# An order for the row sums of the last attention pairs, three ties on VectorE, and two store queues in attention followed by two MLPs

## Chip, cores and metric

The kernel runs on 1 core of one Trainium2 chip. The metric is the device time of an execution in microseconds (us), the median of several runs.

## What is computed

Causal attention over 4 batches x 8 heads x 576 positions x 64 columns, with a cumulative bias on the scores, then an MLP with a leaky activation (its slope alpha is per hidden column), then an MLP with a squared ReLU. All in float32.

```
scores = scale * q @ k.T + minimum(-(cum_i - cum_j), 0), masked causally      # cum = cumsum(max(s, 0))
attn = exp(scores - max); attn = attn / (sum(attn) + 1e-9); out = attn @ v
x = out as [2304, 512]
h = x @ w_in;  g = max(h, 0) + alpha * min(h, 0);  x = g @ w_out               # 512 -> 2048 -> 512
h = x @ w_in2; r = max(h, 0);  g = r * r;          out = g @ w_out2            # 512 -> 2048 -> 512
```

A float32 matmul is made of three matmuls with operands split into a hi part (a cast on ScalarE) and a lo part (source minus hi, on VectorE): hi x hi, hi x lo, lo x hi (TERMS). So nearly every operand costs a cast and a VectorE subtraction, and a matmul with the lo part needs both.

## The kernel before

**Attention.** The 16 pairs of heads run as a software pipeline. PIPE lists 81 small steps with an offset in pairs; RAMP shifts single steps of single pairs by a fraction of a period; the sorted list is emitted step by step, and in_order() ties each instruction to the one before it on its engine, so that in this part every engine's order, SyncE's and GpSimd's included, is the written one. For a pair's row sums the steps are: fin (add eps, ScalarE), rec (line 438, reciprocal on VectorE), spr (line 443, a transpose on TensorE), v_spr (line 448, copy to SBUF on ScalarE), ds (lines 453 and 454, two stores to DRAM from SyncE), di (line 460, two broadcast loads into iv, which has a single buffer), nrm (lines 468 and 470, multiply x by iv on GpSimd). xa and xb (lines 524 and 540) are the products with v; both use one PSUM bank, so xb waits for the eviction of xa (line 278, ScalarE), which stands behind v_spr on ScalarE. After the step tr_4b of the last pair, 24 matmuls of the first MLP (early) are emitted.

**First MLP.** Three passes (c) of 768 tokens, each of 16 hidden blocks (f) of 128. From here the planner orders each engine's instructions by a timeline of its own; dependencies and explicit ties bind it. A step has 24 matmuls h = x @ w_in in two halves of 384 tokens (mlp_mm, line 591; each half has one PSUM bank, which the next step's same half takes over), the activation (mlp_act: lines 610 and 611 on VectorE for each half, then a cast and a subtraction of gs, lines 613 and 614), and, a step later, 24 matmuls of g @ w_out (mlp_out, line 874). Splits of the weights (lines 566 and 567) and conversions of weights for later (conv: lines 115 and 116 on ScalarE, 119 and 120 on VectorE, 124 on GpSimd, with scratch tiles cv_g and cv_t) run beside it, fed by loads of line 92. At the end of the last pass the order of f is 3 to 15, then 0, 1, 2; at f = 15 a list of eleven closures (x_steps: seven splits xc and four differences of x) is made, and in each later step of the loop up to four are taken from it. After the loop, what is left of it runs.

**Second MLP.** Three passes, each with a first product (stage1, line 996, seven products in Strassen's manner, with squares on GpSimd at line 1007) and a second product (Stage2, line 1126). Stage2 has 28 items (i, q): seven products i in the order 1, 5, 6, 2, 7, 4, 3, four q each. An item is 18 matmuls of 256 columns and needs a split th of g (split2, lines 910 and 911, three buffers). Items of i = 6, 7 and 4 (items 8 to 11, 16 to 19 and 20 to 23 of a pass) first need a difference of g in place, on VectorE (lines 1076, 1078, 1080); line 1031 makes one more at the end of stage1. In run, prepare(n + 2) is traced before item n's matmuls, and from n = 3 on every second item is followed by one step of x_steps for the next pass (none in the last). The results are stored by store (lines 1091, 1096, 1099); the last ones of the kernel are those of (mh, h) = (0, 1) with p = 2, in four issues.

`with tc.issue_after(a):` keeps each instruction traced in the block behind a in the order of a's engine. It adds no semaphore.

Of the kernel before, what the change touches and what calls it, by code (L numbers as in the profile page):

```python
# [19 lines left out]
def attention_then_two_mlps(  # L20
# [15 lines left out]
    P = 128  # L36
# [397 lines left out]
    def recip(n):  # L434

        sums = sums_of.pop(n)
        rs = rs_[n % 2][:, 0 : 2 * NT].rearrange("p (i h) -> p i h", h=2)
        nc.vector.reciprocal(rs, sums)
# [162 lines left out]
    def mlp_act(f, ph, first_block=False):  # L601
# [14 lines left out]

    gg_first = pp_.tile([P, HT], F32, name="gg_first")
# [136 lines left out]
    def emit(op, n):  # L754

        nonlocal lastpv, early, lasttr
# [46 lines left out]
        elif what == "rec":  # L803
            recip(n)
# [27 lines left out]
    RAMP = {("qk_10", 0): -0.911, ("qk_11", 0): -0.911, ("red_10", 0): -0.911, ("red_11", 0): -0.911, ("exp_10", 0): -0.911, ("exp_11", 0): -0.911, ("qk_00", 0): -0.964, ("red_00", 0): -0.964, ("qk_01", 0): -0.964, ("red_01", 0): -0.964, ("exp_00", 0): -0.964, ("exp_01", 0): -0.964, ("pp_q0", 2): 0.309, ("pp_q1", 2): 0.309, ("e_q0", 2): 0.309, ("e_q1", 2): 0.309, ("tr_3a", 0): -0.232, ("tr_3b", 0): -0.232, ("v_tr_3a", 0): -0.232, ("v_tr_3b", 0): -0.232, ("pp_k0", 2): 0.185, ("pp_k1", 2): 0.185, ("e_k0", 2): 0.185, ("e_k1", 2): 0.185, ("ppt", 3): -0.16, ("e_qt", 3): -0.182, ("v_xa", 4): -0.203, ("xb", 4): -0.181, ("exp_41", 4): -0.478, ("qk_40", 4): -0.478, ("qk_41", 4): -0.478, ("red_40", 4): -0.478, ("red_41", 4): -0.478, ("exp_40", 4): -0.478, ("qk_20", 4): 0.081, ("red_20", 4): 0.081, ("qk_21", 4): 0.081, ("red_21", 4): 0.081, ("exp_20", 4): 0.081, ("exp_21", 4): 0.081, ("tr_2b", 4): 0.031, ("v_tr_2b", 4): 0.031, ("tr_2a", 4): 0.031, ("v_tr_2a", 4): 0.031, ("e_kt", 3): -0.299, ("pp_k0", 4): -0.261, ("pp_k1", 4): -0.261, ("e_k0", 4): -0.261, ("e_k1", 4): -0.261, ("pp_q0", 4): 0.232, ("pp_q1", 4): 0.232, ("e_q0", 4): 0.232, ("e_q1", 4): 0.232, ("dk", 4): 0.103, ("lq", 3): 0.439, ("tr_2b", 0): -0.116, ("v_tr_2b", 0): -0.116, ("tr_2a", 0): -0.116, ("v_tr_2a", 0): -0.116, ("pp_k0", 1): -0.506, ("pp_k1", 1): -0.506, ("e_k0", 1): -0.506, ("e_k1", 1): -0.506, ("tr_4a", 0): -0.216, ("v_tr_4a", 0): -0.216, ("tr_4b", 0): -0.216, ("v_tr_4b", 0): -0.216, ("qk_10", 1): -0.054, ("qk_11", 1): -0.054, ("red_10", 1): -0.054, ("red_11", 1): -0.054, ("exp_10", 1): -0.054, ("exp_11", 1): -0.054, ("di", 2): -0.214, ("hi_k", 3): -0.711, ("exp_41", 2): -0.016, ("qk_40", 2): -0.016, ("qk_41", 2): -0.016, ("red_40", 2): -0.016, ("red_41", 2): -0.016, ("exp_40", 2): -0.016, ("lk", 2): 0.822, ("lw", 3): 0.44, ("ds", 1): 0.576, ("di", 3): -0.321, ("ppt", 2): 0.09, ("fin", 0): 0.036, ("v_spr", 1): 0.137, ("qk_20", 0): -0.121, ("red_20", 0): -0.121, ("qk_21", 0): -0.121, ("red_21", 0): -0.121, ("exp_20", 0): -0.121, ("exp_21", 0): -0.121, ("qk_10", 4): -0.044, ("qk_11", 4): -0.044, ("red_10", 4): -0.044, ("red_11", 4): -0.044, ("exp_10", 4): -0.044, ("exp_11", 4): -0.044, ("qk_20", 1): -0.084, ("red_20", 1): -0.084, ("qk_21", 1): -0.084, ("red_21", 1): -0.084, ("exp_20", 1): -0.084, ("exp_21", 1): -0.084, ("qk_00", 2): 0.032, ("red_00", 2): 0.032, ("qk_01", 2): 0.032, ("red_01", 2): 0.032, ("exp_00", 2): 0.032, ("exp_01", 2): 0.032, ("e_qt", 2): 0.056, ("ds", 2): 0.204, ("tr_4a", 3): -0.018, ("v_tr_4a", 3): -0.018, ("tr_4b", 3): -0.018, ("v_tr_4b", 3): -0.018, ("tr_2b", 2): 0.086, ("v_tr_2b", 2): 0.086, ("tr_2a", 2): 0.086, ("v_tr_2a", 2): 0.086, ("pp_k0", 3): 0.038, ("pp_k1", 3): 0.038, ("e_k0", 3): 0.038, ("e_k1", 3): 0.038}  # L832
# [25 lines left out]
    po = {}  # L858
# [3 lines left out]
    def mlp_out(c, f, gs, ws):  # L862
# [7 lines left out]
        for m in range(NKB):  # L870
# [91 lines left out]
    g_t = {}  # L962
# [22 lines left out]
    def stage1(stream, fill):  # L985
# [38 lines left out]
        def end(q):  # L1024
# [181 lines left out]
    for f in handed:  # L1206
        f()
# [59 lines left out]
```

## Time and profile before

| | us |
|---|---|
| median of 3 runs | 980.57 (979.06 to 980.58) |
| profiled execution | 979.85 |
| its span, first to last instruction | 978.1 |
| TensorE matmul busy | 954.1 |
| VectorE busy | 773.7 |
| ScalarE busy | 547.6 |
| GpSimd busy | 339.1 |

In the profile PE is TensorE's matmuls, PEld its weight loads, DVE VectorE, ACT ScalarE, POOL GpSimd, SPq and ACTq the DMA issues of SyncE and ScalarE. A row of a timeline has start, duration, engine, line, operation, output<-input; in brackets how long the engine had stood idle before it and what ended that. A row of the waits has who waited for whom, the total, the count and the longest. Attention runs to about 196 us, the first MLP to 608, the second in passes from 608, 733 and 855 to 973.

### The profile page before, as it was taken

Reading aid. Unit: us, or ns where it says so; the run is one execution under the profiler, and the core shown is the slowest. Engines: PE = TensorE matmul, PEld = TensorE weight load, DVE = VectorE, ACT = ScalarE, POOL = GpSimd, SP = SyncE. Lnnn points to the kernel's source line nnn. Section 1 sums busy time; section 2 is a strip of 40 time slices with the busy share of each in tenths; the row PEclk is TensorE's granted clock in tenths of the full one; section 3 lists DMA queues with packets and bytes.
Section 4 is the critical chain, followed back from the end, with each engine's and each line's share of the span. In section 5 each row is a group of like instructions: output and inputs, shape, how many; then the busy total and the mean of one; then the engine's idle time right before and its main releaser. Section 6 shows DMA issues by size and latency. Waiting matters only on the chain.

```text
span 978.1 us, 17664 instructions
## 1 busy us (share of the span) xinstructions
PE 954.1 (98%) x6451; PEld 899.7 (92%) x6451; DVE 773.7 (79%) x1399; ACT 547.6 (56%) x1152; POOL 339.1 (35%) x341
## 2 busy tenths in 40 slices
PE   7999999979999999999999999999999999999997
PEld 6888888869999999999999998998999999999997
DVE  7788878859888887778988768789967889677874
ACT  6999888835555543345645434565535645357442
POOL 7465644124333364442252310443003540035300
PEclk9999999999999999999999999999999999999999
DMA  5777754323444343434644532676544875448473
GB/s 150 190 192 206 191 148 128 83 90 130 129 129 129 101 160 139 144 124 147 233 160 130 183 119 101 185 251 239 179 172 148 290 236 191 171 124 267 138 240 132
DMA packets 107242, 161.39 MB, mean 165 GB/s; under 512 B 31730, under 2 KB 80498, under 8 KB 101778
## 3 DMA queue, kind: packets, MB, share of 16 engines
q1 hardware_dynamic: 106704, 159.89, 52.3%
q8 instruction: 51, 0.84, 0.4%
q10 hardware_dynamic: 450, 0.37, 0.1%
q14 instruction: 37, 0.30, 0.1%
HBM read 121.85 MB, written 30.11 MB: 155 GB/s over the span
## 4 chain that ended last, share of the span: by engine, by line
PE 87%; DVE 6%; DMA 3%; SPq 1%; issue 1%; ACT 1%; POOL 0%; ACTq 0%; POOLq 0%; DVEq 0%
PE ph L591 19%; PE po L874 18%; PE acc L1126 16%; PE b L996 5%; PE a L996 5%; PE ps_tr L490 5%; PE c L996 4%; PE ps_xa L524 2%; PE ps_sc L382 2%; PE ps_xb L540 2%; PE d L996 2%; PE ps_sc L383 2%; PE ps_tr L311 2%; PE ps_sc L388 2%; DVE xc L911 1%
## 5 line engine op out<-in xcount | busy, mean ns | idle before, releaser
L591 PE MATMUL ph<-xs,wi_hi 128*128 128x384 f32 x768 | 196.5, 336 | 5.7 <-DVE gg L611 5.7
L1126 PE MATMUL acc<-w2s,th 128*128 128x256 f32 x1512 | 186.5, 285 | 5.2 <-ACT th L910 3.7
L1126 PEld LDWEIGHTS acc<-w2s,th 128*128 128x128 f32 x1512 | 184.8, 193 | 6.4 <-ACT th L910 4.1
L874 PE MATMUL po<-gs,wo_hi 128*128 128x512 f32 (+1 forms) x768 | 167.6, 337 | 1.1 <-DVE xT L281 1.1
L591 PEld LDWEIGHTS ph<-xs,wi_hi 128*128 128x128 f32 x768 | 136.6, 188 | 8.3 <-DVE gg L611 6.4
L874 PEld LDWEIGHTS po<-gs,wo_hi 128*128 128x128 f32 x768 | 122.0, 189 | 15.5 <-DVE xT L281 1.3
L591 PE MATMUL ph<-xs,wi_lo 128*128 128x384 f32 x384 | 128.8, 335 | 0.0
L910 ACT CAST th<-g 128x768 fp32r<-128x768 f32 x84 | 69.8, 835 | 75.3 <-PE acc L1126 57.3
L911 DVE TENSOR_TENSOR th<-g,th 128x768 fp32r<-128x768 f32 x84 | 82.1, 983 | 25.2 <-ACT th L910 25.1
L613 ACT CAST gs<-gg 128x768 fp32r<-128x768 f32 (+1 forms) x48 | 39.8, 830 | 108.4 <-DVE gg L611 108.2
L874 PE MATMUL po<-gs,wo_lo 128*128 128x256 f32 (+1 forms) x384 | 99.5, 336 | 0.0
L124 POOL TENSOR_TENSOR wc<-cv_t,wc 128x512 uint32<-128x512 uint32 x32 | 47.5, 1487 | 143.5 <-DVE cv_t L120 98.1
L911 DVE TENSOR_TENSOR w1h<-w1f,w1h 128x512 fp32r<-128x512 f32 (+1 forms) x96 | 71.0, 746 | 23.1 <-ACT w1h L910 22.4
L1007 POOL TENSOR_TENSOR g<-g 128x384 f32<-128x384 f32 x24 | 22.2, 923 | 173.2 <-ACT g L1006 169.6
L610 DVE TENSOR_SCALAR gg<-ph,alpha_sb 128x384 f32<-128x384 f32 x95 | 58.0, 611 | 25.4 <-PE ph L591 25.0
L124 POOL TENSOR_TENSOR wf<-cv_t,wf 128x512 uint32<-128x512 uint32 x32 | 45.8, 1433 | 89.2 <-DVE cv_t L120 72.2
L910 ACT CAST w1h<-w1f 128x512 fp32r<-128x512 f32 (+1 forms) x96 | 53.6, 565 | 41.0 <-PE b L996 21.0
L614 DVE TENSOR_TENSOR gs<-gg,gs 128x768 fp32r<-128x768 f32 (+1 forms) x48 | 47.2, 983 | 37.0 <-ACT gs L613 37.0
L409 DVE CUSTOM_DVE_ANT_0 pr<-ps_sc,mask 128x128 f32<-128x128 f32 (+3 forms) x128 | 61.8, 486 | 14.8 <-PE ps_sc L383 11.8
L566 ACT CAST wi_hi<-wf 128x512 fp32r<-128x512 f32 x46 | 28.6, 622 | 78.7 <-PE ph L591 76.1
L591 PEld LDWEIGHTS ph<-xs,wi_lo 128*128 128x128 f32 x384 | 72.4, 188 | 0.1
L422 ACT ACTIVATE pr<-pr,nmax 128x128 f32<-128x128 f32 (+3 forms) x128 | 71.2, 557 | 0.4
(163 smaller groups left out, 2029.6 us busy)
## 6 DMA issues: line engine op xcount, KB each, us to landing
w2s<-w2D SPq DMA_DIRECT2D x42, 1024.0 KB
w1f<-w1D SPq DMA_DIRECT2D x72, 256.0 KB
raw_w<-in_moe_w_in_dram SPq DMA_DIRECT2D x32, 512.0 KB
w2D<-whl SPq DMA_DIRECT2D x16, 896.0 KB
raw_w<-in_moe_w_out_dram SPq DMA_DIRECT2D x24, 512.0 KB
w1D<-wc SPq DMA_DIRECT2D x8, 896.0 KB
iv<-sD SPq DMA_DIRECT2D x32, 144.0 KB
raw_q<-in_q_dram SPq DMA_DIRECT2D x16, 256.0 KB
```

Of the source, the lines that this page charges most:

```text
L124: nc.gpsimd.tensor_tensor(d, tt, d, ALU.add)
L409: nc.vector.tensor_tensor_reduce(o, banks.pop(("s", i, h))[:, :w], m, -1.0, first, ALU.add, ALU.min, nmax[:, h : h + 1])
L422: nc.scalar.activation(o, o, AF.Exp, bias=m, scale=-1.0, accum_out=sums_of[n][:, i, h : h + 1])
L490: last = nc.tensor.transpose(ps[:, z * P : (z + 1) * P], pr[:, c0 : c0 + P], ident)
L591: nc.tensor.matmul(ph[h][:, :HT], ws[a][:, kb * P : (kb + 1) * P], xs[kb][:, bb, h * HT : (h + 1) * HT], start=(cnt == 0), stop=(cnt == 3 ...
L610: nc.vector.tensor_scalar(x, ph[h][:, :HT], 0.0, alpha_sb[:, f : f + 1], ALU.min, ALU.mult)
L614: sub = nc.vector.tensor_sub(z[:, 1], a, z[:, 0].bitcast(F32))
L874: nc.tensor.matmul(acc, ws[a][:, m * P : (m + 1) * P], gs[:, bb, c_], start=first_ and z == 0, stop=lst and z == 2, skip_group_check=True,)
L910: a = nc.scalar.copy(dst[:, 0], src)
L911: v = nc.vector.tensor_sub(dst[:, 1], src, dst[:, 0].bitcast(F32))
L996: nc.tensor.matmul(pt[:, :HT], hl[:, a, c0 + kb * P : c0 + (kb + 1) * P], xc[i][:, b, kb, :], start=(first and cnt == 0), stop=(cnt == 5), ...
L1126: nc.tensor.matmul(acc[tb // 2][:, (tb % 2) * 256 : (tb % 2 + 1) * 256], th[:, x, qq, tb * P : (tb + 1) * P], ws[:, y, (2 * q + qq) % 4, : ...
```

## The change

Six edits. (1) RAMP has four more entries: di of pair 14 stands 0.57 of a period earlier, which is ahead of ds of pair 15 on SyncE; nrm 14 and di 15 and nrm 15 move up with it. (2) early is emitted after the turn (spr) of the last pair instead of before it. (3) In mlp_act, the lines 610 and 611 of a half are tied behind line 611 of the half before (behind the last reciprocal for the first). (4) A difference of g for an item of Stage2 is tied behind line 911 of the split of the item two before it. (5) Of the last stores, two of four are issued from ScalarE. (6) What is left of the eleven closures after the first MLP's loop is tied behind the last evictions on both engines. last_g is new and stores line 1031's instruction.

```diff
     def recip(n):
-        nc.vector.reciprocal(rs, sums)
+        return ins_of(nc.vector.reciprocal(rs, sums))
...
     def mlp_act(f, ph, first_block=False):
         for h in range(2):
             x = halves[h]
-            nc.vector.tensor_scalar(x, ph[h][:, :HT], 0.0, alpha_sb[:, f : f + 1], ALU.min, ALU.mult)
-            nc.vector.scalar_tensor_tensor(x, ph[h][:, :HT], 0.0, x, ALU.max, ALU.add)
+            with tc.issue_after(last_gg[0] or lastrec):
+                nc.vector.tensor_scalar(x, ph[h][:, :HT], 0.0, alpha_sb[:, f : f + 1], ALU.min, ALU.mult)
+            last_gg[0] = ins_of(nc.vector.scalar_tensor_tensor(x, ph[h][:, :HT], 0.0, x, ALU.max, ALU.add))
...
         elif what == "rec":
-            recip(n)
+            lastrec = recip(n)
...
-    RAMP = {..., ("e_k1", 3): 0.038}
+    RAMP = {..., ("e_k1", 3): 0.038, ("di", 14): -0.57, ("nrm", 14): -0.4, ("di", 15): -0.98, ("nrm", 15): -0.89}
...
-        if (op, n) == ("tr_4b", NP - 1):
+        if (op, n) == ("spr", NP - 1):
             early = mlp_mm(xs, first[0])
...
     def mlp_out(c, f, gs, ws):
-                    evac(xT[c][:, m, c_], acc, (m + z) % 2)
+                    last_out[(m + z) % 2] = evac(xT[c][:, m, c_], acc, (m + z) % 2)
...
             if q % 2:
-                nc.vector.tensor_sub(gq[:, :, 1], gq[:, :, 1], gq[:, :, 0])
+                last_g[0] = ins_of(nc.vector.tensor_sub(gq[:, :, 1], gq[:, :, 1], gq[:, :, 0]))
...
         def prepare(self, n):
-                if i == 6:
-                    nc.vector.tensor_sub(gq[:, :, 1], gq[:, :, 3], gq[:, :, 1])
-                elif i == 7:
-                    nc.vector.tensor_sub(gq[:, :, 0], gq[:, :, 1], gq[:, :, 0])
-                elif i == 4:
-                    nc.vector.tensor_sub(gq[:, :, 2], gq[:, :, 2], gq[:, :, 1])
+                if i in (6, 7, 4):
+                    a, b, c = {6: (1, 3, 1), 7: (0, 1, 0), 4: (2, 2, 1)}[i]
+                    with tc.issue_after(self.subs[-2]):
+                        nc.vector.tensor_sub(gq[:, :, a], gq[:, :, b], gq[:, :, c])
                 th = pools["m2"].tile([P, 2, 2, HT], F32R, name="th", tag="th", bufs=3)
                 self.last = split2(th, gq[:, :, PLACE[i]])
+                self.subs.append(self.last[1])
...
         def store(self, mh, h, y, tbs=range(3)):
+            e = nc.scalar if (mh, h) == (0, 1) else nc.sync
             for tb in tbs:
                 if rows[1] == rows[0] + TAIL:
-                    nc.sync.dma_start(out[rows[0] : rows[0] + P, cs], src)
+                    (e if tb == 2 else nc.sync).dma_start(out[rows[0] : rows[0] + P, cs], src)
                     continue
                 for z, r0 in enumerate(rows):
-                    nc.sync.dma_start(out[r0 : r0 + TAIL, cs], src[z * TAIL : (z + 1) * TAIL])
+                    (e if z else nc.sync).dma_start(out[r0 : r0 + TAIL, cs], src[z * TAIL : (z + 1) * TAIL])
...
-    for f in handed:
-        f()
+    with tc.issue_after(last_out[0]), tc.issue_after(last_out[1]):
+        for f in handed:
+            f()
```

## Rows read from the trace of the kernel before

**Rows 1.** The page: busy time of each engine, share of the span, instructions

```profile
PE 954.1 (98%) x6451; PEld 899.7 (92%) x6451; DVE 773.7 (79%) x1399; ACT 547.6 (56%) x1152; POOL 339.1 (35%) x341
```

**Rows 2.** TensorE's waits: who for whom, us in total, times, longest

```profile
PE ph L591 <- DVE gg L611: 5.7, 2, 4.2
PE acc L1126 <- ACT th L910: 3.7, 2, 1.8
...
PE acc L1126 <- DVE th L911: 1.5, 2, 0.8
PE po L874 <- DVE xT L281: 1.1, 1, 1.1
PE ps_xb L540 <- ACT xT L278: 0.9, 1, 0.9
```

**Rows 3.** Three stretches: us, busy time by engine (instructions), PEclk, DMA share, GB/s

```profile
221.10:224.50 3.40, 3.40 (x12) 3.21 (x11) 3.33 (x5) 3.04 (x6) 1.33 (x1) 0.50 0.28 100
...
685.30:688.70 3.40, 3.40 (x18) 3.40 (x17) 3.40 (x5) 1.73 (x3) 0.00 (x0) 0.51 0.00 0
...
690.00:733.00 43.00, 43.00 (x357) 43.00 (x357) 32.49 (x41) 19.39 (x26) 0.00 (x0) 1.00 0.60 199
```

**Rows 4.** Timeline of TensorE behind attention: start, us, instruction, idle before

```profile
207.18 0.62 PE L591 MATMUL ph<-xs,wi_hi 128*128 128x384 f32 x2 [1.51 <-DVE gg L611]
...
211.28 1.32 PE L874 MATMUL po<-gs,wo_hi 128*128 128x512 f32 x6
...
220.01 0.62 PE L591 MATMUL ph<-xs,wi_hi 128*128 128x384 f32 x2 [4.21 <-DVE gg L611]
```

**Rows 5.** Timeline of VectorE in the same stretch

```profile
205.71 0.62 DVE L610 TENSOR_SCALAR gg<-ph,alpha_sb 128x384 f32<-128x384 f32 x1 [3.29 <-PE ph L591]
...
206.58 1.02 DVE L611 SCALAR_TENSOR_TENSOR gg<-ph,gg 128x384 f32<-128x384 f32 x2
...
210.86 0.55 DVE L614 TENSOR_TENSOR gs<-gg,gs 128x384 fp32r<-128x384 f32 x1
...
215.66 0.43 DVE L119 TENSOR_SCALAR cv_t<-cv_g 128x512 uint32<-128x512 uint32 x1 [3.92 <-POOL wf L124]
...
219.41 0.55 DVE L611 SCALAR_TENSOR_TENSOR gg<-ph,gg 128x384 f32<-128x384 f32 x1
```

**Rows 6.** Timelines of GpSimd and of SyncE's queue in the same stretch

```profile
195.07 0.60 POOL L470 TENSOR_TENSOR xT<-xT,iv 128x192 f32<-128x192 f32 x1
206.70 1.01 POOL L468 TENSOR_TENSOR xT<-xT,iv 128x384 f32<-128x384 f32 x1 [11.03 <-DMA iv<-sD]
...
214.33 1.30 POOL L124 TENSOR_TENSOR wf<-cv_t,wf 128x512 uint32<-128x512 uint32 x1
...
202.92 6.91 SPq L460 DMA_DIRECT2D iv<-sD  x4
```

**Rows 7.** Timeline of VectorE at the end of pass 2 of the first MLP

```profile
606.38 0.95 DVE L911 TENSOR_TENSOR xc<-x,xc 128x768 fp32r<-128x768 f32 x1
```

**Rows 8.** Timelines of VectorE, GpSimd and TensorE at the start of Stage2, pass 0

```profile
677.98 0.95 DVE L1078 TENSOR_TENSOR g<-g 128x768 f32<-128x768 f32 x1
678.85 1.58 DVE L1076 TENSOR_TENSOR g<-g 128x768 f32<-128x768 f32 x1
...
682.95 0.95 DVE L1031 TENSOR_TENSOR g<-g 128x768 f32<-128x768 f32 x1
...
678.36 1.25 POOL L1007 TENSOR_TENSOR g<-u 128x384 f32<-128x384 f32 x1 [3.65 <-ACT u L1006]
...
684.87 5.34 PE L1126 MATMUL acc<-w2s,th 128*128 128x256 f32 x30 [1.83 <-ACT th L910]
```

**Rows 9.** Timelines of DMA issues: SyncE behind the last matmul, ScalarE at the start

```profile
973.49 1.11 SPq L1099 DMA_DIRECT2D out_dram<-k  x2
974.70 0.53 SPq L1096 DMA_DIRECT2D out_dram<-k  x1
...
1.23 0.48 ACTq L251 DMA_DIRECT2D raw_k<-in_k_dram  x1
```

More of the change, by code (lines that the diff above doesn't have):

```diff
@@ L615, in mlp_act @@
         return gs, ins_of(act), ins_of(sub)
+    last_gg, lastrec = [None], None
     gg_first = pp_.tile([P, HT], F32, name="gg_first")
@@ L754, in emit @@
     def emit(op, n):
-        nonlocal lastpv, early, lasttr
+        nonlocal lastpv, early, lasttr, lastrec
         what, _, a = op.partition("_")
@@ new lines, in attention_then_two_mlps @@
+    RAMP = {("qk_10", 0): -0.911, ("qk_11", 0): -0.911, ("red_10", 0): -0.911, ("red_11", 0): -0.911, ("exp_10", 0): -0.911, ("exp_11", 0): -0.911, ("qk_00", 0): -0.964, ("red_00", 0): -0.964, ("qk_01", 0): -0.964, ("red_01", 0): -0.964, ("exp_00", 0): -0.964, ("exp_01", 0): -0.964, ("pp_q0", 2): 0.309, ("pp_q1", 2): 0.309, ("e_q0", 2): 0.309, ("e_q1", 2): 0.309, ("tr_3a", 0): -0.232, ("tr_3b", 0): -0.232, ("v_tr_3a", 0): -0.232, ("v_tr_3b", 0): -0.232, ("pp_k0", 2): 0.185, ("pp_k1", 2): 0.185, ("e_k0", 2): 0.185, ("e_k1", 2): 0.185, ("ppt", 3): -0.16, ("e_qt", 3): -0.182, ("v_xa", 4): -0.203, ("xb", 4): -0.181, ("exp_41", 4): -0.478, ("qk_40", 4): -0.478, ("qk_41", 4): -0.478, ("red_40", 4): -0.478, ("red_41", 4): -0.478, ("exp_40", 4): -0.478, ("qk_20", 4): 0.081, ("red_20", 4): 0.081, ("qk_21", 4): 0.081, ("red_21", 4): 0.081, ("exp_20", 4): 0.081, ("exp_21", 4): 0.081, ("tr_2b", 4): 0.031, ("v_tr_2b", 4): 0.031, ("tr_2a", 4): 0.031, ("v_tr_2a", 4): 0.031, ("e_kt", 3): -0.299, ("pp_k0", 4): -0.261, ("pp_k1", 4): -0.261, ("e_k0", 4): -0.261, ("e_k1", 4): -0.261, ("pp_q0", 4): 0.232, ("pp_q1", 4): 0.232, ("e_q0", 4): 0.232, ("e_q1", 4): 0.232, ("dk", 4): 0.103, ("lq", 3): 0.439, ("tr_2b", 0): -0.116, ("v_tr_2b", 0): -0.116, ("tr_2a", 0): -0.116, ("v_tr_2a", 0): -0.116, ("pp_k0", 1): -0.506, ("pp_k1", 1): -0.506, ("e_k0", 1): -0.506, ("e_k1", 1): -0.506, ("tr_4a", 0): -0.216, ("v_tr_4a", 0): -0.216, ("tr_4b", 0): -0.216, ("v_tr_4b", 0): -0.216, ("qk_10", 1): -0.054, ("qk_11", 1): -0.054, ("red_10", 1): -0.054, ("red_11", 1): -0.054, ("exp_10", 1): -0.054, ("exp_11", 1): -0.054, ("di", 2): -0.214, ("hi_k", 3): -0.711, ("exp_41", 2): -0.016, ("qk_40", 2): -0.016, ("qk_41", 2): -0.016, ("red_40", 2): -0.016, ("red_41", 2): -0.016, ("exp_40", 2): -0.016, ("lk", 2): 0.822, ("lw", 3): 0.44, ("ds", 1): 0.576, ("di", 3): -0.321, ("ppt", 2): 0.09, ("fin", 0): 0.036, ("v_spr", 1): 0.137, ("qk_20", 0): -0.121, ("red_20", 0): -0.121, ("qk_21", 0): -0.121, ("red_21", 0): -0.121, ("exp_20", 0): -0.121, ("exp_21", 0): -0.121, ("qk_10", 4): -0.044, ("qk_11", 4): -0.044, ("red_10", 4): -0.044, ("red_11", 4): -0.044, ("exp_10", 4): -0.044, ("exp_11", 4): -0.044, ("qk_20", 1): -0.084, ("red_20", 1): -0.084, ("qk_21", 1): -0.084, ("red_21", 1): -0.084, ("exp_20", 1): -0.084, ("exp_21", 1): -0.084, ("qk_00", 2): 0.032, ("red_00", 2): 0.032, ("qk_01", 2): 0.032, ("red_01", 2): 0.032, ("exp_00", 2): 0.032, ("exp_01", 2): 0.032, ("e_qt", 2): 0.056, ("ds", 2): 0.204, ("tr_4a", 3): -0.018, ("v_tr_4a", 3): -0.018, ("tr_4b", 3): -0.018, ("v_tr_4b", 3): -0.018, ("tr_2b", 2): 0.086, ("v_tr_2b", 2): 0.086, ("tr_2a", 2): 0.086, ("v_tr_2a", 2): 0.086, ("pp_k0", 3): 0.038, ("pp_k1", 3): 0.038, ("e_k0", 3): 0.038, ("e_k1", 3): 0.038, ("di", 14): -0.57, ("nrm", 14): -0.4, ("di", 15): -0.98, ("nrm", 15): -0.89}
@@ L856, in attention_then_two_mlps @@
     ps_o = part1.enter_context(tc.tile_pool(name="ps_o", bufs=1, space=PSUM, reuse_waits="tile"))
-    po = {}
+    po, last_out = {}, {}
     ORD = [list(range(NF))] * (NPASS - 1) + [list(range(NPRE, NF)) + list(range(NPRE))]
@@ L960, in w2_slab @@
         return t
-    g_t = {}
+    g_t, last_g = {}, [None]
     W1_ORDER = []
@@ L1061, in __init__ @@
             self.items = [(i, q) for i in ORDER2 for q in range(NQ // 2)]
-            self.th, self.slab, self.done = {}, {}, 0
+            self.th, self.slab, self.done, self.subs = {}, {}, 0, []
         def fetch(self, i, hq):
```

1 line of the change is left out of this document (removed).

## The prediction

> **What bounds the kernel now.** I read the page first, then TensorE's waits, then the timelines around each wait. TensorE is busy 954.1 us of 978.1 [rows 1] and its chain of waits is short [rows 2]: some 11 us have another engine as their cause after the start, and they stand in four places. From 224.5 us to 602 us TensorE never stops, so an edit there can only lose. The places are: (A) the turn from attention to the first MLP, 200.8 to 220 us, where it waits 0.95 us for an eviction and 1.51 and 4.21 us for the activation of a half (gg, line 611); (B) the end of pass 2 at 606.6 us, 1.07 us for an eviction; (C) the start of the second product in pass 0 and again in pass 1, in all 3.7 us for ScalarE's split and 1.5 us for VectorE's (the pass that has no next x to prepare, the last, shows no such wait); (D) the last stores behind the last matmul. After the 4.21 us wait and after the first of the waits in C the granted clock stands at 0.50 and 0.51 for 3.4 us each [rows 3], the 1.2 GHz level.
>
> The wall of the change is therefore: A 6.67, B 1.07, C 5.13, the two slow stretches, and D. Two slow stretches lose at most half of 3.4, 1.7 us each; by the matmul count, 18 in 3.4 us against 357 in 43.0 us (0.120 each), it is 1.2. I take **1.5 each**.
>
> **A, the first two edits.** Why is gg late? Two causes, both in the rows. First, VectorE's order [rows 5]: the first step of gg for step 1 stands at 205.71, after 3.29 us of idling for its matmuls, *ahead* of the second step of the half before it, at 206.58. The older half's own first step came before that idling, and its bank is what TensorE waits for until 207.18 [rows 4]. Tying each half's first step behind the last half's second puts it into the idle time: the 1.51 us go. Second, GpSimd [rows 5, 6]: at 215.66 VectorE has stood 3.92 us before the second conversion step, because the sum of line 124 that frees its scratch tile runs only at 214.33, behind both last norms; and the gg steps that free TensorE at 220.01 are queued behind that instruction. The norms wait for their DMAs: SyncE issues all four loads of inverse sums in one row from 202.92 on, since the stores of pair 15 stand ahead of pair 14's loads, and those stores wait for the turn, which TensorE does after the 24 early matmuls.
>
> After the change: pair 14's loads go ahead of pair 15's stores, and issue when the norm of pair 13 leaves the single buffer, 195.67. From the second load's issue (203.46 in the row's stretch, half a microsecond into it) to the norm at 206.70 are 3.2 us; so issue 195.8, the norm 199.6 to 201.6. The turn comes before the early matmuls, so both stores are out by about 199, well before pair 15's loads at 201.7; its norm ends at 207.3 where it ended at 214.3. Seven microseconds of GpSimd are freed ahead of line 124. The four issues on SyncE's queue are only reordered; behind them wait the weight loads of line 92, which go earlier too. The transpose of the turn is the same one, moved, so TensorE pays nothing. The copy behind it runs under the early matmuls, and so does the eviction queued behind that copy on ScalarE, which was the 0.95 us. So 6.67 us and one slow stretch are gone, and I ask what is late next: the split activation gs of step 0. TensorE would be at its matmuls, 211.28 in the trace [rows 4], 2.46 us earlier, at 208.8. VectorE's last part of gs ends at 211.41; its run from 205.71 on starts 0.95 earlier and is shorter by the one 0.55 us instruction pulled ahead: 209.9. I charge **1.0 us** of new wait. Bounds: 0 if the weight splits fill the former idle time, and 3 if the next pair of gg steps (1.2 us) and GpSimd's overlap come in front. A = 6.67 + 1.5 - 1.0 = **7.2** (5 to 8.4).
>
> The tie costs nothing later: in the steady steps the second half's matmuls end 2 us after the first's, so the order is the one that stands there anyway. The tie of the first half to the reciprocal of pair 15 adds nothing, as the early matmuls now come behind that pair's turn.
>
> A rule speaks against moving the norms. In the trace a difference of two tiles on VectorE, 0.95 us otherwise, took 1.58 us beside a GpSimd product [rows 8]. The Trainium skill, "SBUF — State Buffer", section "Who interferes with whom", says that a VectorE instruction with two SBUF inputs and a GpSimd instruction that reads SBUF exclude each other for the whole instruction; the trace agrees by that 0.6 us. By it, pair 15's norm, now at 205.7 to 207.3 amid VectorE's busiest stretch, would cost up to two such delays, 1.2 us, and A would be 6.0.
>
> **C, the ties of the differences.** In pass 0, TensorE stops 0.70 us for item 6's split and then 1.83 us, until 684.87, for item 7's [rows 8]. VectorE isn't idle there: between 675 and 686 it runs six differences, for items 8, 9, 10, 16, 17 and 18, among them line 1078 at 677.98 (item 16) and line 1076 at 678.85 (item 9, 1.58 us, beside GpSimd). Line 1031, on which item 7's cast waits, is issued at 682.95 although GpSimd's product for it ended at 679.61. A difference for item m may now come only behind item m-2's split. Item 8's may stand behind item 6's, the other five not before item 7's. Four of the six stand ahead of line 1031, three at 0.87 us from start to start and one at 1.5 with the overlap: 4.1 us leave its front, and it can follow GpSimd at about 680; cast and split then end at 681.8, and the hi part is wanted at 681.9, when items 4 to 6 run through at 18 x 0.120 = 2.17 us each. Both waits go, in pass 1 alike.
>
> The differences don't vanish; they come where splits are due. No semaphore is added: a difference stands in VectorE's own order behind a split that waits for ScalarE's cast, which waits for one of three buffers; behind it are queued the next split and what prepares the next x. From 690 to 733 us VectorE is busy 32.5 of 43 us [rows 3]; six more at 0.95 make 38.2. Locally it is tight. Items 8 to 23 hold 16 splits, 12 differences, 8 steps for the next x and 6 sums of 0.55: 36 x 0.87 + 3.3 = 34.6 us, against TensorE's 16 x 2.17 = 34.7. With two items of lead less a cast and a split, 2.5 us, that holds; at 0.95 a piece it misses by 0.3. The last pass has no x steps, 28 x 0.87 + 3.3 = 27.7: no wait. I charge **0.7 us** over both passes. C = 5.13 + 1.5 - 0.7 = **5.9** (3 to 6.6).
>
> **D, the stores.** Behind the last matmul stand four issues on SyncE; the last pair starts at 973.49 (two in 1.11 us) and 974.70 (0.53) [rows 9]. Two of the four go to ScalarE's queue, which is empty by then. An issue there took 0.48 us at the kernel's start. So the last issue ends near 974.1 and not 975.23: **1.1 us** (0.5 if ScalarE's issue takes the 1.1 us that another at the start took). Passes 0 and 1 take the first branch of store, which is unchanged.
>
> **B, the last tie: nothing.** The eleven steps of x_steps are handed out four to a step of the loop, and three steps follow the one that makes them (f = 0, 1, 2): 12 places for 11. The list is empty when the tied loop starts. The 1.07 us, caused by the split at 606.38 [rows 7] between two evictions, stays. last_g is set and read nowhere. Bounds -1.07 to +1, since the planner lays every engine's order anew.
>
> **Sum**, against the profiled execution's 979.85 (span 978.1 and 1.75 around it): 7.2 + 5.9 + 1.1 = 14.2, giving 965.65. The median of the runs, 980.57, is 0.72 above that execution, so **966.3**.
>
> **The rivals.** (1) *The turn keeps a stall.* VectorE's backlog, not GpSimd, is the bound: for it, 1.0 us of wait came out of my own order; against, the 3.29 and 3.92 us that VectorE idles there [rows 5]. If TensorE still stops 3.5 us and the clock falls, A gives 3.2: 970.4. (2) *Line 1031 is late for another cause*, the chain sum, ScalarE, GpSimd; for it, the cast's wait names line 1031 and no difference; against, the 3.3 us between product and line 1031. C gives 1: 971.2. Both: 975.2. (3) *The planner's order comes out as before* where it matters, since a tie only sets a lower bound: 978.6 to 982.5. (4) *Slower: VectorE becomes the bound of the second product.* 36 pieces at s us in items 8 to 23, less the lead: at s = 1.1 it is 42.9 - 34.7 - 2.5 = 5.7 us late in each of two passes, with two slow stretches 14.4; less A and D, 986.7. It decides from s = 1.03, where the loss eats A and D. For it, 1.58 us beside GpSimd; against, GpSimd has no work at all from 690 to 733 [rows 3].
>
> **How the numbers follow.** Forecast, 963 to 968.5: 0.62. Rival 1 or 2 alone, 968.5 to 973: 0.20; both: 0.05; rival 3: 0.05; rival 4: 0.08. Faster by over 0.2% (2 us, about what a measurement of this kernel tells from no change): 0.87; within: 0.05; slower: 0.08. The lower end is all of A, C and D with no new wait, 964.7, and B's gap gone with it, 963.6, less spread; the range 963 to 974 leaves out rivals 3 and 4, half of "both", and a few hundredths below.
>
> **What would show it.** Right: no wait for gg at 205 to 220 and none for th at 680 to 685 and 803 to 808; the granted clock 1.00 from 26 to 973; line 124's first sum near 208; two stores on ScalarE's queue, SyncE's end about 1 us earlier behind the last matmul; the 1.07 us at the end of pass 2 still there. Wrong: a new wait for gs near 209, or for th in items 16 to 23.

## The result, and the profile of the changed kernel

| | before | after |
|---|---|---|
| median of the runs, us | 980.58 (979.06 to 981.55) | 966.94 (965.37 to 968.26) |
| profiled execution, us | 979.85 | 967.17 |
| its span, us | 978.1 | 965.4 |
| end of the last matmul, us | 973.07 | 961.27 |

The ratio of after to before is 0.9862, with an interval of 0.9842 to 0.9881. The forecast, 966.3 us, was met within 0.7 us, and faster was the likeliest case. The sum is right partly by luck, though: one term was too small, a small one was forecast as nothing, and a loss of 3.9 us that the text didn't see took their gains back. Against the profiled execution, for which the sum was made, it missed by 1.5 us (965.65 forecast, 967.17 measured).

TensorE's waits (who waits for whom, total us, times, longest) are to be read beside [rows 2]:

```profile
PE ph L591 <- DVE gg L612: 1.7, 1, 1.7
PE ph L591 <- DVE xs L578: 1.4, 2, 0.8
...
PE po L876 <- DVE xT L281: 0.5, 1, 0.5
```

(From line 637 on, a line of before has a number two higher in after; line 611 is now 612, and 910 and 911 are 912 and 913.) The waits of acc for th have gone, 5.2 us in all in [rows 2]; the waits for gg fell from 5.7 to 1.7; the wait of ps_xb is gone; po's fell from 1.1 to 0.5. One line behind the start is new: ph waits twice for xs.

**The turn.** TensorE's timeline (start, us, instruction, idle before it) has the place of [rows 4]:

```profile
206.11 1.33 PE L876 MATMUL po<-gs,wo_hi 128*128 128x512 f32 x6
209.14 0.62 PE L591 MATMUL ph<-xs,wi_hi 128*128 128x384 f32 x2 [1.69 <-DVE gg L612]
...
211.33 0.51 PE L876 MATMUL po<-gs,wo_hi 128*128 128x512 f32 x2
```

A wait near 209 was forecast, 1.0 us for gs; it came at 209.14, 1.69 us, for gg. Step 3 of the first MLP (the early matmuls are step 0), which started at 227.98 in before, starts at 220.61: 7.37 us earlier, of which 0.35 are already there when the early matmuls start. The change doesn't touch what stands ahead of them but for one transpose; over the twelve profiled executions of this document's kernels they start anywhere from 195.46 to 196.33 us.

GpSimd (answers to [rows 6]) and SyncE's queue show the mechanism as forecast:

```profile
199.09 1.01 POOL L468 TENSOR_TENSOR xT<-xT,iv 128x384 f32<-128x384 f32 x1 [3.75 <-DMA iv<-sD]
...
204.48 1.01 POOL L468 TENSOR_TENSOR xT<-xT,iv 128x384 f32<-128x384 f32 x1 [3.84 <-DMA iv<-sD]
205.45 1.05 POOL L470 TENSOR_TENSOR xT<-xT,iv 128x192 f32<-128x192 f32 x1
206.47 1.73 POOL L124 TENSOR_TENSOR wf<-cv_t,wf 128x512 uint32<-128x512 uint32 x1
...
195.36 1.08 SPq L460 DMA_DIRECT2D iv<-sD  x2
196.55 0.67 SPq L453 DMA_DIRECT2D sD<-rT  x1
197.26 0.61 SPq L454 DMA_DIRECT2D sD<-rT  x1
200.67 1.13 SPq L460 DMA_DIRECT2D iv<-sD  x2
```

Pair 14's loads go at 195.36, ahead of pair 15's stores at 196.55, and no longer in one row of four from 202.92. Its norm stands at 199.09 instead of 206.70, and line 124's first sum at 206.47 instead of 214.33 (near 208 was forecast).

**The start of the second product, pass 0.** VectorE, the answer to [rows 8]:

```profile
676.02 0.95 DVE L1033 TENSOR_TENSOR g<-g 128x768 f32<-128x768 f32 x1
676.89 0.95 DVE L1080 TENSOR_TENSOR g<-g 128x768 f32<-128x768 f32 x1
677.93 0.96 DVE L913 TENSOR_TENSOR th<-g,th 128x768 fp32r<-128x768 f32 x1
678.80 0.95 DVE L1080 TENSOR_TENSOR g<-g 128x768 f32<-128x768 f32 x1
679.67 0.95 DVE L913 TENSOR_TENSOR th<-g,th 128x768 fp32r<-128x768 f32 x1
680.54 0.95 DVE L1080 TENSOR_TENSOR g<-g 128x768 f32<-128x768 f32 x1
```

Line 1031 (now 1033) starts at 676.02 instead of 682.95, ahead of the differences. These (line 1080) and the splits (line 913) alternate, where [rows 8] has two differences in a row ahead of line 1031; and TensorE has no wait left there, in either pass.

**The new place.** At the end of pass 0 of the first MLP, TensorE's timeline and a stretch (us, busy by engine, PEclk, DMA share, GB/s):

```profile
328.80 0.33 PE L591 MATMUL ph<-xs,wi_hi 128*128 128x384 f32 x1
329.92 0.44 PE L591 MATMUL ph<-xs,wi_hi 128*128 128x384 f32 x1 [0.79 <-DVE xs L578]
...
331.31 0.44 PE L591 MATMUL ph<-xs,wi_hi 128*128 128x384 f32 x1 [0.60 <-DVE xs L578]
...
332.50:335.90 3.40, 3.40 (x12) 3.40 (x11) 3.40 (x7) 2.51 (x4) 0.00 (x0) 0.50 0.01 5
```

The first split of the next pass's x is late, twice, and then the granted clock stands at 0.50, the 1.2 GHz level, for 3.4 us, as it did behind the waits of [rows 3]; at 221.1 and at 685.3 us it is now 1.00.

**The gain by places**, from the starts of the same matmuls in both traces (a difference of differences, so what a wait does to the matmuls and the clock behind it is in it):

| stretch | gain, us | forecast |
|---|---|---|
| start, before the turn | 0.35 | 0 |
| A, the turn (to step 3) | 7.0 | 7.2 |
| end of pass 0 (step 16 to 17) | -3.86 | 0 |
| B, end of pass 2 | 0.6 | 0 |
| C, second product, pass 0 | 3.9 | 5.9 with pass 1 |
| C, pass 1 | 3.5 | |
| the last pass | 0.2 | 0 |
| D, behind the last matmul | 0.88 | 1.1 |
| sum (span) | 12.6 | 14.2 |

The span fell by 12.7, 1.5 less than the sum. The rest of the way to the forecast is the spread of the runs: after's median lies 0.23 us below its profiled execution, where before's lay 0.72 above.

### The profile page after: what moved, and what is told of

Its sections match the earlier page's. It is cut to its first block, busy times and chain, and to the rows that moved or that the text cites. A ratio compares the mean times of both kernels' runs of the same rounds, so it can differ in the third digit from the quotient of the medians.

```text
span 965.4 us, 17665 instructions
## 1 busy us (share of the span) xinstructions
PE 953.2 (99%) x6451; PEld 899.7 (93%) x6451; DVE 773.4 (80%) x1399; ACT 547.5 (57%) x1152; POOL 334.7 (35%) x341
## 4 chain that ended last, share of the span: by engine, by line
PE 80%; DVE 11%; issue 3%; ACT 2%; DMA 2%; SPq 1%; POOL 1%; ACTq 0%; DVEq 0%; POOLq 0%
PE acc L1128 18%; PE ph L591 14%; PE po L876 13%; PE a L998 5%; PE b L998 5%; PE c L998 5%; PE ps_tr L490 5%; PE ps_xb L540 3%; PE d L998 3%; PE ps_xa L524 2%; PE ps_sc L382 2%; PE ps_sc L383 2%; PE ps_tr L311 2%; PE ps_sc L388 2%; DVE gg L611 2%
## 5 line engine op out<-in xcount | busy, mean ns | idle before, releaser
L876 PE MATMUL po<-gs,wo_hi 128*128 128x256 f32 (+1 forms) x768 | 167.0, 336 | 0.5 <-DVE xT L281 0.5
```

Source lines behind the costliest of these rows:

```text
L876: nc.tensor.matmul(acc, ws[a][:, m * P : (m + 1) * P], gs[:, bb, c_], start=first_ and z == 0, stop=lst and z == 2, skip_group_check=True,)
```

## The experiments

Kernels built on before do one part of the change alone; kernels built on after add something to all six. Each time is beside the kernel before of the same batch of runs.

**The turn alone** (edits 1 and 2). The edit is the four new entries of RAMP and

```diff
-        if (op, n) == ("tr_4b", NP - 1):
+        if (op, n) == ("spr", NP - 1):
```

> The kernel before with edits 1 and 2 alone (loads of pair 14 ahead of the stores of pair 15; the turn ahead of the early matmuls). Theory: GpSimd's lateness behind the last two norms is the cause of the 4.21 us wait, so line 124's first sum comes near 207 and not 214, the 4.21 and the 0.95 us go and the slow stretch behind them too; VectorE's order of the halves is untouched, so a wait of about 1.5 us for gg near 205 to 208 stays: 4.5 to 7 us faster than before. Rival, the order of gg on VectorE is the cause of both waits: at most 1.5 us faster, and a wait of 3 us or more for gg between 205 and 220 is still there.

Measured: 972.67 us (971.83 to 975.02), ratio 0.9932 (0.9908 to 0.9955); that is 7.75 us below its before, more than the 4.5 to 7 expected. Its waits, and two rows of VectorE:

```profile
PE acc L1126 <- ACT th L910: 3.3, 2, 1.8
...
PE ph L591 <- DVE xs L578: 1.4, 2, 0.8
PE ph L591 <- DVE gg L611: 1.2, 1, 1.2
...
203.00 0.55 DVE L611 SCALAR_TENSOR_TENSOR gg<-ph,gg 128x384 f32<-128x384 f32 x1
204.02 0.62 DVE L610 TENSOR_SCALAR gg<-ph,alpha_sb 128x384 f32<-128x384 f32 x1 [0.47 <-PE ph L591]
```

Step 3 starts 8.1 us earlier than in before, 7.5 of them behind the start of the early matmuls. So the first two edits give all of A: the second step of a half (203.00) now comes ahead of the first step of the next (204.02) without a tie. Without edit 3 the wait for gg is 1.2 us, less than the 1.69 of after. The wait for xs at the end of pass 0 is here too, so it comes from the turn and from no other edit. It costs 2.3 us here, against 3.86 in after: the two waits are about equally long (0.83 and 0.59; 0.79 and 0.60), but here the granted clock stays at 1.00 behind them. The difference, **1.5 us, is what one half-clock stretch of 3.4 us costs**, as the prediction had estimated it. (From the starts of the matmuls in after's slow stretch itself it comes out at 1.6.)

**The activations' tie alone** (edit 3).

```diff
...
+            with tc.issue_after(last_gg[0] or lastrec):
+                nc.vector.tensor_scalar(x, ph[h][:, :HT], 0.0, alpha_sb[:, f : f + 1], ALU.min, ALU.mult)
+            last_gg[0] = ins_of(nc.vector.scalar_tensor_tensor(x, ph[h][:, :HT], 0.0, x, ALU.max, ALU.add))
```

> The kernel before with edit 3 alone (both steps of gg of a half tied behind the half before). Theory: the 1.51 us wait goes, but GpSimd's two norms still hold line 124 until 214, VectorE's conversion waits for it with gg queued behind, so a wait of 3 us or more and a slow stretch stay: 0 to 2.5 us faster. Rival, the order is the cause: 5 us or more faster, no wait over 1.5 us behind attention.

Measured: 976.44 us (973.65 to 978.74), ratio 0.9962 (0.9948 to 0.9976). VectorE and GpSimd:

```profile
213.89 1.29 POOL L124 TENSOR_TENSOR wf<-cv_t,wf 128x512 uint32<-128x512 uint32 x1
...
215.21 0.43 DVE L119 TENSOR_SCALAR cv_t<-cv_g 128x512 uint32<-128x512 uint32 x1 [3.97 <-POOL wf L124]
```

With GpSimd as late as before (213.89; 214.33 in [rows 6]), VectorE idles 3.97 us (3.92 in [rows 5]) and TensorE still stops 3.83 us for gg, with the granted clock at 0.50 from 218.3 to 221.7 behind it. By the starts of matmuls the tie brings 1.2 us at the turn. The rest of its 2.9 us of span lies elsewhere: 0.45 are there at the start, the wait at the end of pass 2 falls from 1.07 to 0.45, and the second MLP, whose order the planner lays anew, gains 2.8 up to the end of pass 0 and gives 1.7 back in pass 1; 0.5 go at the end of pass 0 of the first MLP. So it is edit 3, and not edit 6, that moved B.

**The differences' tie alone** (edit 4).

```diff
...
+                if i in (6, 7, 4):
+                    a, b, c = {6: (1, 3, 1), 7: (0, 1, 0), 4: (2, 2, 1)}[i]
+                    with tc.issue_after(self.subs[-2]):
+                        nc.vector.tensor_sub(gq[:, :, a], gq[:, :, b], gq[:, :, c])
...
```

> The kernel before with edit 4 alone (a difference behind the split of two items before). Theory: early differences on VectorE are what delays line 1031 and the splits of items 6 and 7, so no wait for th is left in passes 0 and 1, and no slow stretch at 685: 6 to 8 us faster. Rival 2 of the prediction, the chain sum, ScalarE, GpSimd makes line 1031 late: at most 1.5 us faster. Rival 4, VectorE becomes the bound: new waits for th in items 16 to 23.

Measured: 972.92 us (972.18 to 974.23), ratio 0.9928 (0.991 to 0.9945). Of the four waits one of 0.50 us is left. TensorE, and line 1031 on VectorE:

```profile
681.96 4.27 PE L1125 MATMUL acc<-w2s,th 128*128 128x256 f32 x32 [0.50 <-ACT th L910]
...
680.03 0.95 DVE L1031 TENSOR_TENSOR g<-g 128x768 f32<-128x768 f32 x1
```

By the starts of matmuls, pass 0 and pass 1 gain 3.5 us each, and the clock stays at 1.00 in both. Rival 2 of the prediction, that line 1031 is late for another cause than the differences ahead of it, falls: nothing else was changed, and it starts at 680.03, the "about 680" of the prediction, instead of 682.95.

**The same tie one item nearer**, on after. If VectorE's throughput were the limit (rival 4), a tie to the previous item would hardly matter, since the instructions are the same; if it is the distance between a split and what is allowed behind it, it would.

```diff
-                    with tc.issue_after(self.subs[-2]):
+                    with tc.issue_after(self.subs[-1]):
```

> The kernel after with each difference of g tied behind the split of the item one before, not two. Theory: two items back leaves room because difference, cast and split of an item (0.95 + 0.83 + 0.95 and two handovers, about 2.9 us) run beside another item's; one back makes them a chain of 2.9 us against TensorE's 2.17 us an item, so in items 8 to 11 and 16 to 23 it falls behind by 0.7 us each, 8 us in a pass less a lead of 2.5 us before each stretch: new waits for th in all three passes, 6 to 12 us slower than the kernel after. Rival, VectorE's throughput alone decides and the distance does not matter: within 1 us of the kernel after.

Measured: 978.54 us (977.8 to 980.81), 11.6 us above after; ratio to before 0.9989 (0.9978 to 1.0). The stretch from 655 to 735 us, first in this kernel, then in after:

```profile
655.00:735.00 80.00, 78.21 (x588) 75.36 (x587) 63.35 (x83) 36.90 (x58) 11.88 (x11) 1.00 0.56 185
```

```profile
655.00:735.00 80.00, 79.93 (x615) 79.53 (x615) 65.53 (x87) 40.16 (x63) 11.86 (x13) 1.00 0.61 201
```

VectorE does *less* in the same time (63.4 us of 80 against 65.5) and TensorE gets through 588 matmuls instead of 615, at an equal clock. The engine that would be the bound has more idle time, not less: so rival 4's mechanism isn't it. That leaves the chain: a difference behind the split of the item just before it, its own cast and split behind that, one item behind the other. Only some 3 us of the loss appear as named waits for th; the rest is spread over 65 places where a matmul starts 0.1 to 0.5 us later than usual behind the one before, 10.4 us in all; after has four such places. Two items back, the chain of one item can lie beside the next one's. That the chain sets the pace is concluded by elimination: the planner also lays TensorE's order a little differently in this kernel (303 matmuls of items in a row where after has 291), and that wasn't separated.

**The stores alone** (edit 5).

```diff
-                    nc.sync.dma_start(out[rows[0] : rows[0] + P, cs], src)
+                    (e if tb == 2 else nc.sync).dma_start(out[rows[0] : rows[0] + P, cs], src)
```

> The kernel before with edit 5 alone (two of the four last stores from ScalarE's queue). Theory: everything up to the last matmul is as before, and from the end of the last matmul to the end of the span it is 0.9 to 1.1 us shorter than the 5.0 us of before, since two of four issues no longer stand in one line; the run times, whose spread is about 2 us, show 0.5 to 1.5 us less. Rival, the last store's landing or the closing waits hide it: 5.0 us again.

Measured: 978.99 us (977.6 to 982.07), ratio 0.9985 (0.997 to 1.0): the time alone hardly tells it from no change (its profiled span is 1.5 us shorter, 0.8 of it from the start), but the trace does. Issues of SyncE and ScalarE behind the last matmul (972.65 us), against [rows 9]:

```profile
972.68 0.34 SPq L1097 DMA_DIRECT2D out_dram<-k  x1
973.08 0.47 SPq L1100 DMA_DIRECT2D out_dram<-k  x1
...
972.69 0.55 ACTq L1100 DMA_DIRECT2D out_dram<-k  x1
973.33 0.53 ACTq L1097 DMA_DIRECT2D out_dram<-k  x1
```

From the last matmul to the end of the span are 3.93 us here, 4.11 in after and 4.99 in before. Edit 5 is worth 0.9 to 1.1 us.

**The activation really kept together**, on after. In after the two steps of step 1's first half are not adjacent on VectorE: 204.23 and 208.54, with three others between them (below). Here those, the splits of wo and the conversion, may only come behind line 612 of that half.

```diff
...
+            while behind and h == 0:
+                tc.add_manual_dep(behind.pop(0), last_gg[0].name, NOSYNC, reason="gg first")
...
```

> The kernel after, with VectorE's conversions, splits of w_out and subtractions of gs of the first two steps tied behind the second step of gg for the first half of step 1. Theory: the 1.69 us that TensorE still waits behind attention (207.4 to 209.1) are the three instructions that stand between the two steps of that half, lengthened beside GpSimd's norm and sum; with them behind it the wait goes, and gs of step 0 is then ready at about 209, when TensorE reaches its matmuls at 209.5: 1 to 2 us off the kernel after. Rival, what was put back is late itself: a wait for gs or wo_lo near 209.5 takes the place of the one removed, 0 to 1 us.

Measured: 967.33 us (966.57 to 967.7), ratio 0.9871 (0.9855 to 0.9888), against 0.9862 for after. Its waits show where the 1.69 us went:

```profile
PE ph L593 <- DVE xs L580: 1.2, 2, 0.6
...
PE po L882 <- DVE gs L620: 0.9, 1, 0.9
PE ph L593 <- DVE gg L614: 0.9, 1, 0.9
```

The wait of 1.69 us for gg is gone, and in its place stand one of 0.9 for gs from 209.4 us on, the one that the prediction had named, and one of 0.9 for gg from 236.5 on. At step 3 this kernel is 0.7 us ahead of after, behind the second wait 0.4 us behind it (both counted from the early matmuls). So the rival held, not the expected 1 to 2 us: reordering moves the wait and doesn't end it. That VectorE has more to do here than TensorE leaves it time for is the likely reading; no run takes work away from VectorE to show it. The two waits for xs are here too (0.62 and 0.60 us), with the granted clock at 1.00 behind them; of the 1.7 us that this spares, 1.6 are lost again in the second MLP.

**The next x ahead of the conversion**, on after. The theory of the new wait: ScalarE's conversion (line 116) writes a buffer, wc, of which there is one; it has to wait until the store of the former content has landed, and the four casts of the next x (line 577), which could run, are queued behind it. ScalarE in before and then in after, the same place in the same order of instructions:

```profile
331.83 0.66 ACT L116 ACTIVATE wc<-raw_w 128x512 uint32<-128x512 uint32 x1 [3.53 <-DMA w1D<-wc]
332.40 2.30 ACT L577 CAST xs<-xT 128x768 fp32r<-128x768 f32 x3
```

```profile
327.01 0.67 ACT L116 ACTIVATE wc<-raw_w 128x512 uint32<-128x512 uint32 x1 [5.67 <-DMA w1D<-wc]
327.58 2.28 ACT L577 CAST xs<-xT 128x768 fp32r<-128x768 f32 x3
```

In before the wait of 3.53 us was paid in slack: TensorE needed the first split at 336.15, and VectorE had it done at 334.69. In after it needs it at 328.80, 7.35 us earlier, while line 116 came only 4.82 earlier: its store was issued 6.2 us earlier (321.87 against 328.04), and L116 started 5.1 us behind it instead of 3.8.

The DMA view shows why. Both lines cover 5.2 us from the store's issue on, in 40 slices of 0.13 us, first in before, then in after:

```profile
GB/s 0 0 0 0 0 0 551 331 441 441 386 496 386 496 276 607 55 772 55 717 165 551 331 0 0 126 0 0 0 0 0 0 0 0 0 0 0 0 0 0
```

```profile
GB/s 0 0 0 0 126 0 496 331 386 441 331 496 331 496 276 551 110 717 55 717 165 551 331 0 55 0 55 0 55 0 0 55 0 55 0 0 0 0 0 0
```

The lone 126 is a packet of 16 KB from the queue that the page calls "q8 instruction". In before it starts when the store is through, in after ahead of the store's first packet; there it takes 1.45 us, and a few of the store's packets come behind all the others, one at a time (the 55s), so that the last one ends 4.57 us behind the issue instead of 3.35. All eight profiled executions of kernels with the turn moved have this packet within the store's time, and their store ends at 3.97 to 5.37 us; the four without the turn have it at the store's end or behind it, and the store ends at 3.21 to 3.74. The other 84 such stores of the twelve executions have no such packet in their time and end at 3.2. No run moved the packet by itself.

A rival of the theory reads the same rows as the planner's new order or as VectorE's backlog; then the splits would stay late with the casts in front. The edit puts the steps of the conversion behind the last cast, at the ends of passes 0 and 1:

```diff
-        nc.scalar.copy(xs[:, 0], xT[c][:, kb, :])
+        last_x[0] = ins_of(nc.scalar.copy(xs[:, 0], xT[c][:, kb, :]))
...
+        turn = f == ORD[c][-1] and c + 1 < NPASS
+        if not turn:
+            run_todo(anchor)
...
+            run_todo(last_x[0])
```

> The kernel after, with one edit more: in the last step of pass 0 and of pass 1 of the first MLP the conversion for later weights is put behind the four casts of the next pass's x on ScalarE. Theory: the new wait of the kernel after at 329 to 331 us, with its slow stretch, comes from those casts being queued on ScalarE behind line 116, which waits for the store of the weight sums to land; with the casts in front both go, 3 to 4 us off the kernel after, about 963. Rival, GpSimd beside VectorE's subtractions of x is the cause: the wait stays and the time is 966 to 968.

Measured: **963.68 us** (962.66 to 966.68), ratio 0.9837 (0.9815 to 0.986). ScalarE:

```profile
323.23 2.31 ACT L579 CAST xs<-xT 128x768 fp32r<-128x768 f32 x3 [2.32 <-PE ph L593]
325.44 0.61 ACT L566 CAST wi_hi<-wf 128x512 fp32r<-128x512 f32 x1
325.96 0.83 ACT L579 CAST xs<-xT 128x768 fp32r<-128x768 f32 x1
326.70 0.66 ACT L115 ACTIVATE cv_g<-raw_w 128x512 f32<-128x512 f32 x1
327.27 0.65 ACT L116 ACTIVATE wc<-raw_w 128x512 uint32<-128x512 uint32 x1
```

The casts run from 323.23 on, 4.35 us earlier than in after; line 116 starts at 327.27, 0.26 us later than in after, and nobody waits for it. TensorE has no wait for xs and no slow stretch; step 17 starts 3.9 us earlier than in after, which is the whole loss. The theory holds, and the rival on record (GpSimd beside VectorE's subtractions of x) falls. At the end of pass 1, where after has no such wait, the same edit loses 1.2 us; the next kernel leaves it out there and loses nothing.

**The same at the end of pass 0 only**, on after: `turn` asks for `c == 0`.

> The kernel after, with the conversion of the last step of pass 0 alone put behind the casts of the next x (x_first did it at the end of pass 1 too, where nothing waited before). Theory: the 3.9 us at the end of pass 0 go and the 1.1 us that x_first lost at the end of pass 1 do not come: 962 to 963.5, under x_first. Rival, the planner lays the work behind it anew and what x_first gained in pass 1's end and behind is part of its 963.7: 963.5 to 965.

Measured: 964.49 us (963.03 to 965.22), ratio 0.9825 (0.9793 to 0.9857). Up to the last output matmul of the first MLP it is 4.6 us ahead of after: 3.8 from the loss at pass 0 undone, with nothing given back in pass 1, and 0.8 that were there behind the turn already, where the two kernels are the same. In the second MLP 2.2 us of that go again, at three waits of 0.4 to 0.6 us for d, b and acc among others; the planner's order there is another one. So the 962 to 963.5 expected did not come, and the rival did. By times it can't be told from the kernel with both (0.8 us apart, in different batches, with overlapping ranges). Both beat before clearly; their medians are 2.5 and 3.3 us below after's, which was measured in another batch.

**Both turns**: the activation kept together and the next x first at pass 0.

> The kernel after with the edit of the run before, and with the conversion of the last step of pass 0 (not of pass 1) put behind the casts of the next x on ScalarE. Theory: the two edits lie in different places and add: 3.5 to 4 us for the casts, as x_first showed in pass 0, without the 1.1 us that it lost at the end of pass 1, and 1 to 2 us for gg: 961 to 963. Rival, they meet in the planner's order of the first MLP and one of them is given back: 963.5 or more.

Measured: 964.75 us (964.26 to 965.74), ratio 0.9847 (0.9833 to 0.9862). Against 961 to 963 expected, that is the kernel above, within its range; keeping the activation together adds nothing here either.

**After once more**, for a second profile.

> The kernel after once more, for a second profile. Theory: the wait for xs at 329 to 331 and the 1.7 us for gg at 207 to 209 are the program's and stand in every execution; the slow stretches of TensorE's clock behind them need not. Rival: the wait for xs is one execution's, from a store that landed late, and is not there in this one.

Measured: 967.10 us. The waits for xs (0.97 and 0.61 us) and the slow stretch behind them (331.2 to 334.7 us) are there again, with L116 starting 5.4 us behind its store's issue; the wait for gg is 1.5 us. So the loss isn't an accident of one execution.

## Point by point

**What bounds the kernel: right.** TensorE is busy 953.2 of 965.4 us, and nearly all that was won is idle time and slow clock of TensorE (the rest, 0.9 us, lies behind its last matmul). The waits that this part lists add up to 12.9 us, not to "some 11". One step of this part said that from 224.5 to 602 us an edit can only lose. That is exactly where the unforeseen loss came, and the sum had no term for it.

**A, right in size, wrong in what is left.** 7.0 us against 7.2. The loads, the norms and line 124 went where the text put them. Two steps of it failed. First, the division between the edits: the text gave the tie of edit 3 the 1.51 us of the first wait for gg. The turn alone takes it all, since the halves then pair up by themselves. Secondly, what is late next: gs was named with 1.0 us, and it is gg, 1.69. VectorE in after:

```profile
204.23 0.62 DVE L611 TENSOR_SCALAR gg<-ph,alpha_sb 128x384 f32<-128x384 f32 x1 [0.47 <-PE ph L591]
204.77 1.27 DVE L120 SCALAR_TENSOR_TENSOR cv_t<-cv_g,cv_t 128x512 uint32<-128x512 uint32 x1
205.97 1.09 DVE L567 TENSOR_TENSOR wo_lo<-wf,wo_hi 128x512 fp32r<-128x512 f32 x1
206.98 1.63 DVE L615 TENSOR_TENSOR gs<-gg_first,gs 128x384 fp32r<-128x384 f32 x1
208.54 0.55 DVE L612 SCALAR_TENSOR_TENSOR gg<-ph,gg 128x384 f32<-128x384 f32 x1
```

The tie sets which half comes first; it doesn't keep other work out from between the two steps of one. The three instructions between them take 0.68, 0.68 and 0.55 us in the kernel that runs them behind line 612; here, beside the norm of pair 15 and line 124 (204.48 to 208.20), they take 1.27, 1.09 and 1.63, 2.1 us more. All three read two tiles of SBUF; line 611, which reads PSUM, keeps its 0.62 beside the norm, and over after's whole trace line 612 (PSUM and one tile of SBUF) takes at most 0.56 us, in the 46 cases beside a GpSimd instruction as in the 50 without one. This agrees with the rule that the prediction set against the change, the Trainium skill, "SBUF — State Buffer", section "Who interferes with whom", by which a VectorE instruction contends with a GpSimd instruction that reads SBUF when it has two SBUF inputs itself. The prediction priced it at two delays and 1.2 us and left it out of its own sum; the rows show three and 2.1. That the wait would be away without these delays wasn't tried by itself: the kernel that ran the three behind line 612, mostly undelayed, got other waits instead, which speaks for rival 1's cause, VectorE's backlog, at 1.7 us rather than at its 3.5, without showing it.

**C, right in mechanism; the term was mis-sized.** 7.4 us against 5.9. The text took the wall from the bracketed idle times, 5.13 us, which count from the modelled end of a matmul. From start to start the four places in before are 0.98, 2.11, 1.05 and 2.11 us where 0.12 is usual: 5.8 us. With 1.5 for the slow stretch it is 7.3, and 7.4 came back. Rival 3, an order as before where it matters, fell with the same rows. (The prediction's 681.8 for "cast and split" is the end of the cast alone by its own durations; the split ends 0.95 us later. The forecast doesn't hang on it.) And the 0.7 us charged for six differences moved into the crowded items 8 to 23 did not come: behind the start of the product TensorE has no wait in either pass. Rival 4's VectorE at its limit was not reached; the kernel tied one item nearer points to the chain's length, and not the sum of the pieces, as the thing to watch.

**B, forecast as nothing, 0.6 us.** That the tie of edit 6 is empty was right: in after the last cast of xc (601.54) and its last split (603.42) both start ahead of the last evictions on their engines (604.22 and 604.29), so nothing stands behind them for the tie to hold. But edit 3 reorders VectorE there as well, inside the bounds of -1.07 to +1 that the text gave to such a reordering.

**D, right.** 0.88 us against 1.1; ScalarE's issues took 0.55 and 0.54 us, near the 0.48 and far from the 1.1 that its start showed.

**What was missed: the end of pass 0, 3.86 us.** The step that failed is "I ask what is late next". It was asked at the turn and not at the next place where TensorE meets a chain that is not its own. The row to look at was in the trace of before: line 116 waits 3.53 us there, four casts stand behind it, and their first split is done 1.5 us before TensorE asks for it. A slack of 1.5 us was on view, and a gain of 7 us upstream was about to be spent on it. The side chain of weight conversions, with its single buffer and its store of 896 KB, went only 4.82 us earlier where TensorE went 7.35, so TensorE gained 2.53 us on it: 1.18 because the store was issued only 6.17 us earlier, and 1.35 because it took longer beside the packet of the instruction queue. For the first split either part alone would have fitted into the slack; together they didn't, and the slow stretch added 1.5 us. The second part could not be read from the trace of before; how much of the loss would be left without it wasn't tried.

**The signs it named.** Of the signs of being right four came (no wait for th, line 124's first sum near 208, two stores on ScalarE's queue, an earlier end of SyncE) and three did not: a wait for gg stands at 207.4 to 209.1, the granted clock is 0.50 at 332.5, and the wait at the end of pass 2 is 0.46 us and not 1.07. So the time was met without the mechanism being right in all its parts.

**The parts don't add up.** By their traces the turn gives 8.0 us of span, edit 3 2.9, edit 4 7.7 and edit 5 1.5: 20.1, where together they give 12.7. By the starts of the same matmuls, 1.8 us of the difference are only the start, where each of the four executions is 0.4 to 0.8 us ahead of before; 1.3 lie at the turn, where edit 3 has nothing left to gain; 0.8 at the end of pass 0, where the loss with all edits is larger than the parts' losses together; and 3.4 in the second MLP, where the turn and edit 3 each took a part of C's waits by another order of the planner.

## What to carry to other kernels

When a change lets the bounding engine through a stall, follow it to every later point where it meets a side chain, and compare the gain with the slack there: a wait that costs nothing today, in front of work that is needed soon, can be the next stall. An instruction that waits for a DMA is better placed behind what else its engine could do in that time, as in the kernel with the casts first, unless that costs elsewhere, as at the end of pass 1. And a tie between two instructions of a chain wants room for the chain's length: the same tie won 7.4 us two items back, and one item back it gave all of that away and 4 us more.

## What the runs showed of the hardware

Behind like waits the granted clock doesn't always fall. At the end of pass 0 it stood at 0.50, the 1.2 GHz level, for 3.4 us behind idle times of TensorE of 0.79 and 0.60 us (after) and of 0.97 and 0.61 us (its second execution), and at 1.00 behind 0.83 and 0.59 us (the turn alone), 0.62 and 0.60 us (the activation kept together) and 1.00 and 0.60 us (the tie one item nearer). One such stretch cost 1.5 us.

VectorE's instructions with two SBUF inputs took up to three times as long beside a GpSimd instruction (1.63 instead of 0.55 us), while line 612, with PSUM and one SBUF tile, took 0.56 us at most either way.

A store of 896 KB had its last packet 3.2 us behind its issue in 84 of 96 cases. With a 16 KB packet of the instruction queue in its time, in eight cases, it was 4.0 to 5.4 us.
